# One buffer for the queries: an attention and MLP kernel whose loads and DMA transposes take turns

## The chip, the cores and the metric

The kernel runs on one core of a Trainium2 chip. Five engines work side by side, each on a queue of instructions in a fixed order: TensorE (PE: matmuls, and PEld its weight loads), VectorE (DVE), ScalarE (ACT), GpSimd (POOL) and SyncE (SP). The last two mainly issue DMAs here, which 16 DMA engines then carry out. An engine runs its instructions in order, and each waits for the semaphores that it names. The metric is the device time of one execution in microseconds (us).

## What is computed

The reference, cut to what matters:

```python
def _attn_ref(q, k, v, p):                      # q, k, v: 8 x 8 x 576 x 64; p: 8 x 8 x 32 x 64
    def sm_attn(qq, kk, vv):
        s = scale * np.matmul(qq, kk.transpose(0, 1, 3, 2))
        s = s - np.max(s, axis=-1, keepdims=True)
        a = np.exp(s)
        a = a / (np.sum(a, axis=-1, keepdims=True) + 1e-09)
        return np.matmul(a, vv)
    p_packed = sm_attn(p, k, v)
    return sm_attn(q, p_packed, p_packed)

def _moe_ref(x, w_in, w_out):                   # x: 4608 x 512; w_in: 512 x 2048; w_out: 2048 x 512
    h = x @ w_in
    g = np.where(h >= 1, h, np.where(h <= -1, 0.0, (h + 1) ** 2 / 4.0))
    return g @ w_out
```

For each of 8 batches 32 landmarks `p` first attend to the 576 keys and values, then the 576 queries attend to the 32 packed rows. The output of the 8 heads, side by side, goes through a two-layer MLP.

## The kernel before

The heads' outputs are never written out. The packed rows of a batch are multiplied with `w_in` at once (`mp`, copied to `M`), so that the hidden layer `h` is `M` times the attention weights `A`. One batch goes through these steps: the keys are turned (`kT`), scores `sp` of landmarks and keys and their exponentials `ex`; packed products `pk` with the values; `mp` and `M`; the queries turned (`qT`), scores `s` and exponentials `eT`, their sums, and the weights `A`; then 16 tiles of `h`, each with an `x`, `t` and `hT` step on ACT and DVE; then output tiles `o` of 128 tokens, 16 matmuls each, copied to `ob` and stored. 36 output tiles go through, 9 for each pair of batches. Much of `o` of one pair runs between the steps of the next batches, and so keeps TensorE busy.

Keys and queries of batches 0 and 1 are turned on TensorE (`tp`). From batch 2 on a DMA transposes them from one buffer of SBUF to another, issued from SP (line 562). For batches 5 to 7 the scores are computed with the landmarks on the partitions, and a third DMA transpose turns the exponentials (`exn` to `ex`, line 642). All loads that change the type from f32 to bf16 are issued from POOL (line 411 and others); stores go out from SP (line 1003), in one queue with the transposes.

Four heads of the first keys come another way: `k_raw`, loaded as f32 from SP and ACT (line 458) and cast on DVE and ACT; the landmarks of two batches come as `p_raw` (line 453), cast to `p_nat`, turned on TensorE (`tpp`) and copied to `pT`, which the first scores need.

The buffers are counted in `BUFS`: two for `q`, one each for `k`, `v` and `vv` (the values in pairs of heads, copied on DVE at line 663), two for `kT` and `qT`. Tiles of one tag share its buffers; whoever writes to one waits until those who used it before are done. `p_raw`, the later landmarks `p_late` and the `vv` tiles share the tag `vv`; `k_raw` has the tag `q`.

The order on each engine is written out as numbers: `ORDER` gives a rank (and an engine) to every task of the class `Plan`, which runs through the tasks with its own estimates of their times and from that emits the instructions engine by engine. `add` for a load on POOL carries how long it holds the queue, when it starts and how much it moves; for SP the same for stores and transposes. `chain` lets a task stand behind the one before it. `chain("crossed", t)` keeps the transposes in order, and loads of the weights and of batches 0 and 1 are chained too; the later ones stand as their ranks say. The string `LOADS` and the loop behind it (line 446) make the loads; where the plan leaves TensorE idle early on, `warm` puts matmuls of zeros.

Of the kernel before, what the change touches and what calls it, by code (L numbers as in the profile page):

```python
# [178 lines left out]
def kernel(  # L179
# [54 lines left out]
    o00 35 40 46 49 70 71 73 74 76 81 87 88 94 98 108 111 64A 6
    o01 36 38 44 53 62 93 101 102 112 114 116 117 118 119 122 125 70A 5
    o02 31 50 54 58 59 64 67 69 77 83 85 90 96 100 104 105 65D 2
    o03 41 43 47 56 60 65 68 75 78 82 86 91 95 97 103 107 66D 9
    a1 32 34D 31A 33 35D 36D 79 59D 51A 80 60D 52A 34 33 39 35 63 47A 46A 56 84 53 89 55 57 63 54 92 56 58 64 72 58D
        50A 99 60A 59A
    h1 109 62 69D 70 113 65 71D 73 106 61 67D 68 115 66 72D 74 121 69 76D 78 127 72 79D 83 126 71 77D 84 135 77 79A 86  # L240
        110 63 67A 75 120 68 81D 85 128 73 80D 82 131 74 78A 89 136 80 88D 90 151 82 85A 94 133 76 83A 93 132 75 87A
        95
    o04 138 140 143 144 145 147 155 158 162 163 166 169 172 174 175 177 89A 7
    o05 124 129 130 137 139 146 152 153 156 157 167 179 182 183 184 185 92A 14
    o06 190 196 197 198 203 208 211 216 218 221 222 224 225 228 231 232 111A 13
    o07 186 187 188 189 191 192 193 194 199 200 201 202 204 205 206 207 97A 12
    o08 123 134 141 148 149 150 154 159 161 165 168 170 171 176 178 180 90A 8
    a2 3 4 160 84 164 86 91 92 173 88A 96D 97 181 91 99 101 103 93 100 102 104 98D 195 94A 96A 95A
    h2 209 98 107D 109 214 102 105A 115 210 99 108D 112 215 103 114D 117 220 106 118D 120 213 101 111D 113 223 108
        124D 126 217 104 116D 119 226 109 122D 127 212 100 110D 123 233 112 119A 132 239 115 129D 131 241 121 122A 133  # L250
        219 107 121D 125 230 114 116A 128 246 120 123A 134
    o10 270 271 272 273 274 275 278 279 280 281 282 295 296 297 303 311 161D 19
    o11 236 237 243 244 249 251 252 253 254 259 261 264 266 268 276 277 141D 17
    o12 227 235 238 242 245 247 248 250 256 257 258 260 262 263 265 267 127A 24
    o13 286 288 290 292 299 300 306 307 308 309 310 312 314 316 318 319 151A 21
    a3 10 11 229 110 234 113 105 106 240 117A 118A 130 255 124 135 137 139 125 136 138 140 126A 269 129A 130A 128A
    h3 291 137 152D 156 287 134 146D 148 302 142 155D 160 283 131 143D 158 284 132 145D 147 294 139 153D 154 301 141
        148A 164 289 135 150D 151 293 138 144A 157 305 145 159D 162 304 143 166D 169 317 149 163D 170 320 150 165D 171
        313 146 153A 167 321 155 156A 172 285 133 136A 149
    o14 326 329 333 335 338 339 341 343 344 350 351 353 355 358 360 363 180D 43  # L260
    o15 403 404 406 407 409 410 411 412 413 416 417 419 420 421 422 423 193A 28
    o16 322 324 325 327 328 330 331 332 334 337 340 342 345 346 347 348 160A 23
    o17 369 370 374 375 376 382 384 387 389 391 392 393 395 398 399 400 199D 26
    o18 352 354 356 357 359 362 364 367 373 378 383 388 405 408 414 415 190A 33
    a4 15 16 298 140 315 147 142 144 323 154A 152A 168 336 157 173 175 176 159 174 177 178 158A 349 163A 162A 161A
    h4 379 173 178A 202 371 169 185D 187 402 185 187A 207 368 168 186D 194 377 172 189D 191 372 170 171A 190 394 182
        198D 206 390 179 195D 196 366 167 182D 183 385 180 181A 201 381 176 191A 213 365 166 184D 188 396 186 196A 212
        386 177 193D 197 397 183 184A 203 380 174 175A 192
    o20 471 472 474 476 480 482 483 485 489 490 491 494 496 498 500 502 224A 37
    o21 463 468 473 479 484 486 487 492 493 497 499 501 503 505 506 507 226A 36  # L270
    o22 428 429 430 431 433 438 440 441 443 444 450 454 458 460 465 466 211A 31
    o23 424 425 426 427 432 434 436 437 439 442 445 446 448 449 452 456 218D 32
    a5 18 20 361 164 165 22 179 181 401 189A 188A 205 418 192 208 209 211 194 210 214 215 195A 435 199A 197A 198A
    h5 488 220 236D 237 464 209 223D 226 469 214 230D 231 477 217 221A 235 461 208 221D 222 462 210 227D 229 504 225
        243D 244 451 202 207A 228 470 213 216A 238 455 204 224D 241 453 203 216D 217 459 206 225D 232 478 218 219A 245
        467 212 227A 246 457 205 219D 220 475 215 228A 247
    o24 532 533 534 535 536 539 540 541 542 543 544 545 547 548 549 550 238A 39
    o25 508 509 510 511 516 517 519 520 521 522 523 524 525 526 528 529 232A 38
    o26 512 513 514 515 527 530 537 546 556 574 575 576 577 578 591 592 256A 41
    o27 552 553 554 555 557 559 560 562 563 566 567 568 569 570 571 572 246A 40  # L280
    o28 579 584 585 586 589 593 595 600 602 603 605 609 610 614 619 621 270A 42
    a6 25 27 447 200 201 29 200 204 481 242D 240D 239 518 229 248 249 253 231 250 252 257 230A 573 264D 248A 247A
    h6 561 243 261D 263 565 244 262D 269 564 245 266D 278 558 242 265D 267 587 254 274D 276 588 258 279D 283 594 257
        277D 281 590 255 260A 280 596 259 264A 284 601 262 282D 287 582 251 270D 272 608 265 289D 290 583 252 273D 275
        617 268 269A 293 580 249 268D 271 618 273 295D 299
    o30 625 626 629 634 635 641 642 643 644 645 646 648 650 651 653 661 284A 45
    o31 652 654 655 657 659 660 662 663 666 673 675 676 678 680 681 683 288A 46
    o32 597 599 607 612 613 615 616 622 624 627 630 631 636 637 639 647 279A 44
    o33 665 667 668 669 670 671 672 674 677 679 682 684 685 686 687 689 290A 47
    a7 30 34 495 222 223 35 233 234 531 233A 234A 251 538 236 256 258 259 235 254 255 260 237A 551 239A 240A 241A  # L290
    h7 598 261 285D 292 640 277 302D 303 638 278 309D 312 606 263 286D 288 649 287 310D 314 658 285 311D 313 623 272
        281A 306 628 280 283A 307 656 282 286A 316 632 275 297D 301 581 250 253A 296 611 266 298D 300 633 276 304D 305
        604 267 274A 308 620 271 291D 294 664 289 315D 317
# [778 lines left out]
```

## Time and profile before

| | |
|---|---|
| three runs | 240.09, 243.59, 240.09 us (median 240.09) |
| profiled execution | 242.46 us, of which the span of its instructions 240.7 |
| granted TensorE clock | 0.999 |
| queue of POOL's loads | 18.25 MB, packets took 51.9% of the 16 engines' span |
| queue of SP's and ACT's DMAs | 17.93 MB, 37.5% |
| output matmuls `o` (line 977) | 608, busy 145.4 us |
| hidden matmuls `h` (line 894) | 512, busy 78.3 us |

The profile is one execution. "Busy" of a matmul counts from its issue to its modelled end, and neighbours overlap; so the share of busy time is high even where matmuls come a little apart, and the pace is read from the chain, which shows start to start. In the timeline and the chain a row begins with its start and its duration; "[x <-Y]" is idle time of the engine ahead of the row and what ended it. In the tables of DMAs the last number of a row is the median time from issue to landing.

### The profile page before, as it was taken

What the parts mean: (1) busy time and instruction counts of PE and PEld (TensorE: products, weight loads), DVE (VectorE), ACT (ScalarE), POOL (GpSimd) and SP (SyncE); (2) the same over time, 40 slices, a digit from 0 to 9 for tenths busy, and PEclk for the clock granted to TensorE, in tenths of its full rate; (3) what the DMA queues carried; (4) which work ended last, traced back from release to release, by engine and by line L of the source; (5) the groups of instructions that cost most, each with busy time, mean ns of one, the idle gap of its engine ahead of it and who ended that gap; (6) DMA issues with size and microseconds to landing.
All of it is one profiled execution on the core that took longest, in us unless ns stands there. A gap on an engine that the chain in (4) does not pass through costs nothing.

```text
span 240.7 us, 5388 instructions
## 1 busy us (share of the span) xinstructions
PE 234.2 (97%) x2126; PEld 132.2 (55%) x2126; DVE 187.3 (78%) x354; ACT 182.7 (76%) x315; POOL 28.1 (12%) x42
## 2 busy tenths in 40 slices
PE   7999999999999999999999999999999999999994
PEld 2556555466554765476536653664445566654454
DVE  3547988589959898979898899597997998977102
ACT  3577887899777999898989989987769989782000
POOL 8453210200020120040011030000000000000000
PEclk9999999999999999999999999999999999999999
DMA  7999999999999999999999979998711110222133
GB/s 157 188 205 208 204 205 206 202 212 207 146 176 246 169 171 230 167 181 198 185 147 176 225 134 191 219 222 157 154 46 44 44 46 5 82 88 71 45 81 112
DMA packets 62505, 37.01 MB, mean 154 GB/s; under 512 B 34576, under 2 KB 58000, under 8 KB 62480
## 3 DMA queue, kind: packets, MB, share of 16 engines
q0 software_dynamic: 23104, 18.25, 51.9%
q1 hardware_dynamic: 38832, 17.93, 37.5%
q10 hardware_dynamic: 544, 0.49, 0.7%
q8 instruction: 16, 0.26, 0.4%
q14 instruction: 9, 0.07, 0.1%
HBM read 37.22 MB, written 9.44 MB: 194 GB/s over the span
## 4 chain that ended last, share of the span: by engine, by line
PE 84%; DMA 9%; ACT 2%; POOL 2%; issue 1%; DVE 1%; SPq 0%; ACTq 0%; DVEq 0%; POOLq 0%
PE o L977 49%; PE h L894 24%; DMA w_in_sb<-in_moe_w_in_dram 5%; DMA out_dram<-ob 4%; PE mp L747 3%; PE pk L680 2%; PE sp L590 1%; PE o L1036 1%; PE s L761 1%; POOL q L411 1%; ACT t L910 1%; PE tp L533 1%; PE pk L695 1%; ACT ob L328 1%; ACT M L328 0%
## 5 line engine op out<-in xcount | busy, mean ns | idle before, releaser
L977 PE MATMUL o<-w_out_sb,hT 128*128 128x512 bf16 (+2 forms) x608 | 145.4, 370 | 0.7 <-DVE hT L915 0.3
L915 DVE SCALAR_TENSOR_TENSOR hT<-t 128x576 bf16<-128x576 f32 (+1 forms) x130 | 92.2, 743 | 7.1 <-ACT t L910 6.4
L900 ACT ACTIVATE x<-h 128x576 f32<-128x576 f32 (+1 forms) x130 | 78.4, 644 | 12.2 <-PE h L894 9.9
L977 PEld LDWEIGHTS <-hT 128*128 128x128 bf16 x608 | 56.2, 98 | 54.1 <-issue 7.0
L894 PE MATMUL h<-A,M 128*128 128x288 bf16 x512 | 78.3, 288 | 0.1
L894 PEld LDWEIGHTS <-M 128*128 128x128 bf16 x512 | 50.1, 98 | 26.4 <-ACT M L328 0.7
L908 DVE TENSOR_SCALAR t<-x 128x576 f32<-128x576 f32 (+1 forms) x88 | 38.1, 452 | 12.1 <-ACT x L900 11.0
L328 ACT COPY ob<-o 128x512 f32<-128x512 f32 x26 | 15.2, 586 | 20.0 <-PE o L977 18.4
L328 ACT CAST M<-mp 128x1024 bf16<-128x1024 f32 (+1 forms) x28 | 26.7, 1002 | 2.9 <-PE mp L747 2.9
L910 ACT ACTIVATE t<-x 128x576 f32<-128x576 f32 (+1 forms) x42 | 28.1, 675 | 0.4
L328 DVE COPY ob<-o 128x512 f32<-128x512 f32 (+2 forms) x12 | 7.2, 599 | 14.0 <-PE o L977 14.0
L411 POOL DMA_DIRECT2D k<-in_k_dram x8 | 6.4, 802 | 76.6 <-DMA kT<-k 71.4
L815 DVE SCALAR_TENSOR_TENSOR A<-eT,rs,rc 128x576 bf16<-128x576 bf16 (+1 forms) x18 | 12.7, 732 | 2.8 <-ACT rc L810 2.6
L784 ACT ACTIVATE eT<-s,rs 128x576 bf16<-128x576 f32 x16 | 11.5, 739 | 2.4 <-PE s L761 2.4
L1036 PE MATMUL o<-zeros 128*128 128x512 bf16 (+1 forms) x42 | 12.1, 408 | 1.2 <-DVE zeros L365 1.2
L747 PE MATMUL mp<-w_in_sb,ppT 64*32 64x512 bf16 x256 | 10.8, 382 | 0.1
L411 POOL DMA_DIRECT2D q<-in_q_dram x10 | 7.5, 753 | 18.5 <-PE tp L533 11.6
L595 ACT ACTIVATE ex<-sp 96x768 bf16<-96x768 f32 (+1 forms) x12 | 8.3, 698 | 1.8 <-PE sp L590 1.5
L794 DVE TRANSPOSE_TENSOR_REDUCE r<-eT 128x18 f32<-128x576 bf16 x12 | 9.1, 755 | 0.3 <-ACT eT L784 0.3
L800 DVE STREAM_TRANSPOSE rc<-r 128x576 f32<-128x576 f32 x12 | 8.9, 754 | 0.1
L328 DVE CAST M<-mp 128x1024 bf16<-128x1024 f32 (+1 forms) x5 | 5.6, 1118 | 4.1 <-PE mp L747 4.1
L411 POOL DMA_DIRECT2D v<-in_v_dram x8 | 6.4, 794 | 13.7 <-DVE vv L663 12.2
(62 smaller groups left out, 113.3 us busy)
## 6 DMA issues: line engine op xcount, KB each, us to landing
v<-in_v_dram POOLq DMA_DIRECT2D x8, 576.0 KB, 11.2
out_dram<-ob SPq DMA_DIRECT2D x23, 192.0 KB, 3.3
k<-in_k_dram POOLq DMA_DIRECT2D x7, 576.0 KB, 9.6
q<-in_q_dram POOLq DMA_DIRECT2D x7, 576.0 KB, 11.9
out_dram<-ob SPq DMA_DIRECT2D x24, 128.0 KB, 2.4
w_out_sb<-in_moe_w_out_dram POOLq DMA_DIRECT2D x4, 512.0 KB, 19.5
w_in_sb<-in_moe_w_in_dram POOLq DMA_DIRECT2D x3, 512.0 KB, 15.1
out_dram<-ob SPq DMA_DIRECT2D x23, 64.0 KB, 3.0
```

What stands on the lines that cost most here:

```text
L328: i = (nc.vector.tensor_copy if e == "DVE" else nc.scalar.copy)(to, of)
L411: G_.dma_start(tokens(nm, b)[:, heads(hs)], rows_of(nm, b, hs))
L747: m = nc.tensor.matmul(have["mp", b, f][a * NP:(a + 1) * NP, g], have["ppT", b][r, g, a], w_in_sb[r, a, f * FW:(f + 1) * FW], start=True, ...
L784: nc.scalar.activation(have["eT", b, g], have["s2", b, g][:, :, :HALF], AF.Exp, scale=rs_of[b][:, g, 1:])
L815: V.scalar_tensor_tensor(have["A", b][:, g, xs], have["eT", b, g][:, xs], rs_of[b][:, g, :1], have["rc", b, g][:, xs], ALU.mult, ALU.mult)
L894: nc.tensor.matmul(have["h", b, fi][:, hf, :HALF], have["M", b][:, g, fi * P:(fi + 1) * P], have["A", b][:, g, hf], start=(g == 0), stop=( ...
L900: nc.scalar.activation(have["x", b, fi][:, hs[0]:hs[-1] + 1], have["h", b, fi][:, hs[0]:hs[-1] + 1, :HALF], AF.Prelu, bias=-1.0, alpha=0.5)
L908: V.tensor_scalar(t, x, 1.0, 0.0, ALU.add, ALU.max)
L910: nc.scalar.activation(t, x, AF.Relu, bias=1.0)
L915: V.scalar_tensor_tensor(dst, t, 1.0, t, ALU.min, ALU.mult)
L977: m = nc.tensor.matmul(have["o", key][:, :w], hT[:, fi, i * P:(i + 1) * P], w_out_sb[:, fi, cols], start=(fi == 0), stop=(fi == KF - 1))
L1036: nc.tensor.matmul(o[:, :w], zeros[:, :P], zeros[:, :w], start=True, stop=True)
```

## The change

The queries get one buffer in place of two, and `k_raw` moves from the queries' tag to `vv`. From batch 2 on every load stands in one chain, in the order queries, values, keys, behind which come the transposes of keys and queries. The identity is no longer held behind the first load of keys. The planner's numbers for SP's transposes, for two loads and for the start are new (how long a transpose takes, what share it leaves to loads beside it), and the whole table `ORDER` is new.

```diff
-        self.free = defaultdict(float, DMA=1.75)
+        self.free = defaultdict(float, DMA=1.95)
...
-            return [(a[0], 1.0 - b[0][3]), (b[0], b[0][3])]
+            return [(a[0], 0.5 if b[0][3] < 0.4 else 1.0 - b[0][3]), (b[0], b[0][3])]
...
-    MB0 = {("k", 0, 4): 0.70, ("v", 0, 0): 1.25, ("q", 0, 0): 0.5}
+    MB0 = {("k", 0, 4): 0.75, ("v", 0, 0): 1.35, ("q", 0, 0): 0.5}
...
     ORDER = """
-    first 0 0 0 1 1D 0A
-    load 0 1 2 3 4 5 6 7 8 9 10 11 12 13 14 15 16 21 17 18 19 22 20 23 26 25 27 24 28 29 30 31 32 34 33 35
+    first 0 0 0 1 0A 1D
+    load 0 1 2 3 4 5 6 7 8 9 10 11 12 13 14 15 16 17 18 19 20 21 22 23 24 25 26 27 28 29 30 31 32 33 34 35
...
-    BUFS = dict(w=3, o=2, k=1, q=2, v=1, vv=1, kT=2, qT=2, ex=2, ks=2, ppT=2, M=2, A=2, eT=4, ln=2, rc=2, x=4, t=4, ob=4)
+    BUFS = dict(w=3, o=2, k=1, q=1, v=1, vv=1, kT=2, qT=2, ex=2, ks=2, ppT=2, M=2, A=2, eT=4, ln=2, rc=2, x=4, t=4, ob=4)
...
-    k_raw = work.tile([TP, 4, NC * D], f32, tag="q", name="k_raw", bufs=BUFS["q"])
+    k_raw = work.tile([TP, 4, NC * D], f32, tag="vv", name="k_raw", bufs=BUFS["vv"])
...
-        if key[0] == "p" or "w" in key[0] or key[1] < 2:
-            chain("load", t)
+        chain("load", t)
...
-        for nm in "kqv" if b == 3 else "qkv":
+        for nm in "qvk":
             load(nm, b)
-
-    identity.behind += landed["k", 0, 4]
...
-    k_first = plan.add("first", {"SP": (1.0, 4.2, load_k_raw)})
-    p_first = plan.add("first", {"SP": (0.5, 3.6, load_p_raw)}, behind=[k_first])
+    k_first = plan.add("first", {"SP": (1.0, 4.9, load_k_raw)})
+    p_first = plan.add("first", {"SP": (0.5, 5.1, load_p_raw)}, behind=[k_first])
...
-            t = plan.add(mine, {"SP": (2.9, 0.0, turn, 3.9, 0.9, 0.27)}, landed[nm, b, 0], [nm + "T"])
+            t = plan.add(mine, {"SP": (3.0, 0.0, turn, 2.4, 1.2, 0.2)}, landed[nm, b, 0], [nm + "T"])
...
-            t = plan.add(mine, {"SP": (1.45, 0.0, turn, 2.1, 0.9, 0.27)}, [ready["ex0"], ready["ex1"]], ["ex"])
+            t = plan.add(mine, {"SP": (1.5, 0.0, turn, 1.6, 1.2, 0.2)}, [ready["ex0"], ready["ex1"]], ["ex"])
```

Three lines fewer stand in the file, so a line of the second half carries a number that is 3 lower after the change.

The head of SP's queue, with what each instruction waits for. DMAHW is the landing of a DMA from SP or ACT, DMASW that of one from POOL; the other names are engines. Before:

```order
L458 DMA k_raw<-in_k_dram 96x2x384
L453 DMA p_raw<-in_p_dram 128x256
L1003 DMA out_dram<-ob 32x512 [waits DVE_49]
L1003 DMA out_dram<-ob 96x512
L562 DMA_TRANSPOSE kT<-k 128x24x96 [waits DMASW3_49,PE_49,Activation_49]
L562 DMA_TRANSPOSE qT<-q 128x24x96 [waits DMASW1_49,PE_49,Activation_49]
```

The same queue after the change:

```order
L455 DMA k_raw<-in_k_dram 96x2x384
L450 DMA p_raw<-in_p_dram 128x256 [waits DMAHW0_49,DMAHW1_49,DVE_49,Activation_49]
L559 DMA_TRANSPOSE kT<-k 128x24x96 [waits DVE_49,DMASW4_49,PE_49,Activation_49]
L559 DMA_TRANSPOSE qT<-q 128x24x96 [waits DVE_49,DMASW2_49,PE_49,Activation_49]
L1000 DMA out_dram<-ob 96x512 [waits Activation_49]
L1000 DMA out_dram<-ob 32x512
```

`p_raw` waited for nothing; now it waits for both loads of `k_raw` and for both engines that cast it. The first two transposes stand ahead of the first store.

The loads on POOL from the queries of batch 1 on. Before:

```order
L411 DMA q<-in_q_dram 96x8x384 [waits DMAHW2_49,DMAHW0_49,DMASW7_49]
L428 DMA w_out_sb<-in_moe_w_out_dram 128x4x512 [waits DMASW0_49]
L411 DMA q<-in_q_dram 96x8x384 [waits DMASW1_49,PE_49]
L433 DMA p_late<-in_p_dram 128x3x256 [waits DMAHW1_49,DMASW2_49,DVE_49]
L411 DMA k<-in_k_dram 96x8x384 [waits DMASW3_49,PE_49]
L411 DMA q<-in_q_dram 96x8x384 [waits DMASW7_49,DMASW4_49,PE_49]
L411 DMA v<-in_v_dram 96x8x384 [waits DMASW5_49]
L411 DMA k<-in_k_dram 96x8x384 [waits DMAHW5_49,DMASW6_49,DMASW3_49]
```

After:

```order
L410 DMA q<-in_q_dram 96x8x384 [waits DMASW7_49,PE_49]
L427 DMA w_out_sb<-in_moe_w_out_dram 128x4x512 [waits DMASW0_49]
L410 DMA v<-in_v_dram 96x8x384 [waits DMASW5_49,DMASW1_49,PE_49]
L410 DMA q<-in_q_dram 96x8x384 [waits DMASW7_49,DMASW2_49,PE_49]
L432 DMA p_late<-in_p_dram 128x3x256 [waits DMAHW1_49,DMAHW0_49,DMAHW2_49,DMASW3_49,DVE_49]
L410 DMA k<-in_k_dram 96x8x384 [waits DMASW4_49]
L410 DMA q<-in_q_dram 96x8x384 [waits DMAHW4_49,DMASW2_49]
L410 DMA v<-in_v_dram 96x8x384 [waits DMASW6_49,DMASW1_49,DVE_49]
L410 DMA k<-in_k_dram 96x8x384 [waits DMAHW3_49,DMASW4_49]
```

The values of batch 2 stand ahead of its queries and keys. The queries of batch 3 waited for TensorE's turning of an earlier batch; now they wait for a DMA from SP, the transpose of the queries of batch 2. Before, the keys of batch 3 were asked for ahead of its values (queries of batch 3, values of batch 2, keys of batch 3); now its queries, values and keys stand together. From there on the three follow each other so to the end.

More of the change, by code (lines that the diff above doesn't have):

```diff
@@ L234 @@
[L234 to L241, printed above, removed]
-        95
@@ L243 @@
[L243 to L293, printed above, removed]
@@ new lines @@
+    o00 33 34 41 50 66 73 74 78 87 93 98 100 119 121 125 126 70A 4
+    o01 31 43 48 56 57 62 68 80 82 88 90 91 92 95 101 109 67D 19
+    o02 37 44 46 53 58 59 70 71 72 79 81 85 103 105 106 107 66D 6
+    o03 32 35 40 52 63 64 75 77 86 96 99 104 108 111 112 113 61A 5
+    a1 36 35D 32A 38 36D 33A 83 50A 59D 84 60D 51A 39 34 45 36 67 51D 48A 54 89 52 94 54 56 64 53 97 55 57 65 76 56D
+        49A 102 59A 58A
+    h1 116 64 73D 75 110 60 68D 69 115 63 72D 74 114 62 70D 71 120 67 76D 79 124 71 74A 84 122 68 78D 81 123 73 82D 85
+        118 66 69A 80 136 76 78A 89 128 72 83D 87 117 65 77D 88 134 75 90D 92 150 82 84A 94 142 79 86A 96 137 77 81A
+        95
@@ new lines @@
+    o04 146 147 149 152 153 156 157 159 164 165 168 170 174 176 177 178 88A 12
+    o05 127 129 133 135 139 145 148 155 158 160 169 171 173 179 180 181 99D 7
+    o06 183 184 188 201 203 210 213 217 219 220 221 222 226 229 230 232 111A 17
+    o07 190 191 192 193 194 195 196 197 198 199 200 202 204 205 206 207 95A 11
+    o08 130 131 132 138 140 143 144 151 154 162 163 166 172 185 186 187 91A 10
+    a2 2 3 161 83 167 85 91 93 175 87A 97D 98 182 89 101 103 105 90 102 104 106 100D 189 94A 93A 92A
@@ new lines @@
+    h2 214 100 104A 118 216 102 119D 122 209 97 110D 112 215 101 115D 121 218 103 123D 126 211 98 113D 116 224 106
+        120D 129 223 105 107A 124 228 109 125D 127 212 99 114D 117 208 96 109D 111 240 116 131D 134 227 110 120A 135
+        233 112 128D 130 225 108 115A 132 244 117 121A 136
+    o10 231 235 237 239 242 246 248 249 251 252 261 265 269 275 276 279 129A 16
+    o11 268 270 271 272 273 274 277 278 280 285 286 289 292 293 294 295 152D 18
+    o12 238 241 243 247 250 253 255 256 257 258 259 260 262 263 264 266 125A 13
@@ new lines @@
+    o13 299 302 303 305 306 308 309 311 314 315 320 321 322 323 324 325 155A 22
+    a3 8 9 234 113 236 114 107 108 245 119A 118A 133 254 122 137 139 141 123 138 140 142 124A 267 128A 127A 126A
+    h3 288 135 153D 154 281 130 145D 146 287 134 136A 156 290 138 141A 158 284 133 149D 150 283 132 147D 148 282 131
+        151D 157 296 139 146A 163 317 152 168D 171 310 147 149A 167 291 137 155D 162 312 148 164D 165 300 144 151A 170
+        298 142 161D 166 319 153 156A 172 297 140 159D 160
+    o14 345 348 349 350 351 353 355 356 359 362 363 365 367 368 369 370 185D 25
@@ new lines @@
+    o15 397 398 400 402 403 405 406 412 414 416 417 418 419 420 421 422 191A 28
+    o16 304 316 318 326 327 328 329 332 334 336 337 338 339 340 341 343 160A 21
+    o17 331 333 335 342 346 347 352 354 377 378 381 385 387 389 391 392 181A 27
+    o18 374 379 382 383 386 394 396 399 404 407 409 410 411 413 415 425 192A 44
+    a4 14 15 301 143 307 145 143 144 313 150A 154A 169 330 157 173 175 177 158 174 176 178 159A 344 161A 162A 163A
+    h4 366 170 194D 195 376 174 175A 201 372 172 191D 192 357 164 182D 188 358 165 180D 184 380 176 196D 198 361 167
+        189D 193 388 182 185A 203 360 166 183D 186 375 179 197D 200 393 184 204D 208 373 173 178A 205 401 186 195A 216
+        384 177 206D 218 390 180 190A 214 371 171 187D 190
@@ new lines @@
+    o20 471 472 474 476 479 480 481 483 486 494 495 497 498 500 503 505 223A 36
+    o21 473 475 477 482 485 487 489 490 492 496 499 501 502 504 506 507 222A 34
+    o22 424 426 427 428 429 430 432 434 435 437 441 443 448 452 454 461 209A 37
+    o23 431 433 436 438 439 440 442 445 446 450 455 457 462 463 465 466 229D 31
+    a5 20 23 364 168 169 24 179 181 395 183A 202D 199 408 187 207 210 213 188 209 211 215 189A 423 194A 212D 193A
+    h5 467 208 213A 236 484 217 241D 242 488 221 245D 247 464 207 218A 248 456 202 225D 226 449 199 223D 235 491 219
+        244D 246 460 206 231D 232 453 201 203A 227 451 200 222D 224 458 204 228D 239 447 198 220D 221 470 211 237D 251
+        459 205 230D 238 493 220 249D 252 468 210 226A 257
@@ new lines @@
+    o24 576 577 581 582 583 584 585 586 589 592 594 595 597 598 601 602 254A 42
+    o25 542 543 545 546 547 549 551 552 554 556 557 558 562 563 568 569 240A 40
+    o26 509 510 511 515 517 519 522 524 526 530 532 540 541 544 548 553 262D 39
+    o27 512 513 514 516 518 520 521 525 527 528 529 531 534 535 537 538 230A 38
+    o28 559 560 561 564 565 566 570 571 572 573 579 588 596 604 605 606 256A 41
+    a6 26 29 444 196 197 30 217 219 469 233D 212A 234 478 216 240 243 254 214 250 253 255 215A 508 224A 229A 225A
@@ new lines @@
+    h6 539 233 261D 272 536 231 234A 271 590 248 249A 283 575 242 273D 277 599 253 284D 286 578 244 245A 275 533 232
+        270D 274 614 260 292D 293 600 255 288D 289 591 250 280D 282 593 251 285D 291 580 246 276D 278 587 247 252A 281
+        616 261 267A 297 574 243 279D 290 608 259 262A 294
+    o30 611 615 618 619 626 627 629 630 635 637 639 640 641 642 643 644 273A 43
+    o31 609 610 612 613 622 623 625 628 633 634 650 651 655 657 663 664 311D 45
+    o32 647 648 649 653 654 656 658 660 661 662 666 668 673 676 678 680 284A 46
@@ new lines @@
+    o33 669 670 671 672 674 675 677 679 681 682 683 684 685 686 687 689 286A 47
+    a7 32 33 523 227 228 35 258 259 550 235A 260D 256 555 236 263 264 268 238 265 267 269 237A 567 241A 239A 266D
+    h7 636 272 302D 303 659 278 280A 312 652 277 309D 310 645 279 314D 318 631 268 270A 299 638 271 304D 306 665 281
+        283A 316 620 263 264A 295 617 276 307D 313 632 269 287A 319 607 257 296D 317 624 265 298D 301 603 258 287D 300
+        646 274 308D 315 667 282 285A 320 621 266 275A 305
+    o34 725 726 727 730 731 732 733 736 738 739 740 741 743 744 745 747 321D 50
@@ L300 @@
+    o35 694 695 698 699 700 701 702 703 705 706 707 708 711 714 715 716 288A 49
+    o36 721 722 723 724 728 729 734 735 737 742 746 748 749 750 751 752 322D 51
+    o37 688 690 691 692 693 696 697 704 709 710 712 713 717 718 719 720 289A 48
+    o38 753 754 755 756 757 758 759 760 761 762 763 764 765 766 767 768 323D 52 769 770 771 772 773 774 775 776 777
+        778 779 780 781 782 783 784 324D 53 785 786 787 788 789 790 791 792 793 794 795 796 797 798 799 800 325D 54
     """
```

18 lines of the change are left out of this document (6 added, 12 removed).

## The prediction

> **What bounds the kernel now.** I read the page's engine rows first, then the stretches of 10 us, the chain that ended last, the timeline of the first 31 us, and the DMA tables.
>
> ```profile
> PE 234.2 (97%) x2126; PEld 132.2 (55%) x2126; DVE 187.3 (78%) x354; ACT 182.7 (76%) x315; POOL 28.1 (12%) x42
> DMA  7999999999999999999999979998711110222133
> GB/s 157 188 205 208 204 205 206 202 212 207 146 176 246 169 171 230 167 181 198 185 147 176 225 134 191 219 222 157 154 46 44 44 46 5 82 88 71 45 81 112
> ```
>
> TensorE is busy for 97% of the span: it is the bound. But the DMA engines are full too, until slice 28 (170 us). So a change of the transfers can hardly gain, since TensorE has nearly no idle time to give back, and it can lose, as soon as a transfer comes after the matmul that needs it. How little there is to gain after the start:
>
> ```profile
> 150.00:160.00 10.00, 9.66 (x80) 6.22 (x80) 7.04 (x14) 8.94 (x18) 0.00 (x0) 1.00 1.27 205
> 170.00:180.00 10.00, 9.65 (x109) 4.37 (x106) 9.66 (x20) 7.10 (x13) 0.00 (x0) 1.00 0.42 107
> ```
>
> The number behind the stretch's length is TensorE's busy time. From 30 to 230 us these two alone stand below 10.00, together 0.69 us. Now the chain (start, duration, what):
>
> ```profile
> 61.75 1.80 PE o L977 x8
> 69.06 0.70 PE pk L680 x24
> 84.72 0.49 PE h L894 x4
> 92.91 1.73 PE o L977 x8
> 162.02 0.70 PE pk L680 x24
> 175.00 0.70 PE pk L680 x24
> ```
>
> It shows two things. The packed products of keys (pk) of batch 2 start at 69.06, of batch 7 at 175.00, 105.9 us for five batches. And 8 output matmuls took 1.80 us at 62 us, but 1.73 at 93: 225 ns and 216 ns each. The profiled execution took 242.46 us (span 240.7 and 1.8 around it), the median of the three runs 240.09. Some 60 us (20 to 80) at 216 for 225 would be 2.4 us shorter, which is the distance between the two; so I take 2.4 us off the sum at the end. The Trainium skill (TensorE: Matmul & The Clock Gate, "Wait — 56ns, not 53.3ns?") gives 215.7 ns from one matmul of 512 columns to the next at the full clock: the row at 93 us agrees, the one at 62 does not, though the granted clock reads 1.00 in both. By the page's pace, which I estimate from that figure, the same 2.4 us come off.
>
> **Part 1, the start.** `k_raw` moves into the buffer of `p_raw`, so the load of the landmarks (`p_raw`) now waits until both casts of `k_raw` are done. The timeline of before:
>
> ```profile
> 1.18 0.43 SPq L453 DMA_DIRECT2D p_raw<-in_p_dram  x1
> 2.07 0.22 POOL masks.py:197 MEMSET ident<- 128x128 bf16 x1
> 2.37 0.29 POOL masks.py:199 TENSOR_SCALAR_AFFINE_SELECT ident<-ident 128x128 bf16<-128x128 bf16 x1
> 5.05 0.83 ACT L328 CAST k<-k_raw 96x768 bf16<-96x768 f32 x1 [3.03 <-DMA k_raw<-in_k_dram]
> 5.27 0.29 DVE L508 CAST p_nat<-p_raw 128x256 bf16<-128x256 f32 x1 [0.19 <-DMA p_raw<-in_p_dram]
> 5.62 0.28 PE L479 MATMUL tpp<-ident,p_nat 128*128 128x128 bf16 x2
> 5.95 1.09 ACT L328 COPY pT<-tpp 64x128 bf16<-64x128 bf16 x4
> 8.34 0.70 ACT L328 COPY kT<-tp 128x288 bf16<-128x288 bf16 x2 [1.30 <-PE tp L533]
> 8.92 0.50 ACT L595 ACTIVATE ex<-sp 96x384 bf16<-96x384 f32 x1
> 9.86 1.41 ACT L595 ACTIVATE ex<-sp 96x384 bf16<-96x384 f32 x3 [0.44 <-PE sp L590]
> 11.46 0.94 PE L685 MATMUL pk<-ex,v 96*64 96x32 bf16 x48
> 19.42 0.41 PE L894 MATMUL h<-A,M 128*128 128x288 bf16 x2
> ```
>
> Before, `p_raw` was issued at 1.18 and was hidden behind the keys. Now it is issued when the cast on ScalarE ends, 5.05 + 0.83 = 5.9. How long it takes there no row shows; the nearest are
>
> ```profile
> out_dram<-ob SPq DMA_DIRECT2D x24, 128.0 KB, 2.4
> p_raw<-in_p_dram SPq DMA_DIRECT2D x1, 128.0 KB, 4.1
> ```
>
> a store of the same size beside loads (2.4) and its own load behind `k_raw` in one queue (4.1). I take 3.0, nearer to the store since nothing is ahead of it in its queue. So it lands at 8.9. Behind it VectorE waits with the cast in its order, and with it the copies of the turned keys; on TensorE the turned landmarks and all that follows. From 8.9: cast 0.29, transposes 0.28, four pT copies 1.09, one kT copy 0.4 (half of 0.70 rounded up), four exponentials 0.50 + 1.41 = 1.9. That ends at 12.9, where before it ended at 9.86 + 1.41 = 11.3: **1.6 us later** (1.0 with 2.4, 2.7 with 4.1), and `pk` follows at once. The identity is made ahead of the first load on the POOL queue: 0.22 + 0.29 us later for `k`, at no cost, since the keys' second half stands behind `tpp` on TensorE, which is now later than that; without `p_raw`'s wait it would cost up to 0.5.
>
> Not all of the 1.6 arrives. The first phase then waits for weights, which come by their own queue:
>
> ```profile
> 12.44 1.55 POOL L423 DMA_DIRECT2D w_in_sb<-in_moe_w_in_dram  x2 [0.33 <-DMA q<-in_q_dram]
> 30.32 0.41 PE L747 MATMUL mp<-w_in_sb,ppT 64*32 64x512 bf16 x8
> DMA to landing us min/median/max: 9.6/13.0/16.8
> ```
>
> (the last row is that of `w_in_sb`.) The second of these loads is issued at 13.25 and takes the 16.8, so it lands at 30.05 and its matmuls start at 30.32. The queue was full at 205 GB/s all the while, so it lands there now too. TensorE's work up to there shifts into that wait. Between nothing and all of 1.6 I take half: **+0.8**.
>
> **Part 2, the loads in a ring.** With one buffer, the queries of a batch are asked for only when the batch before has been transposed, values and keys stand behind them on the POOL queue, and the transposes behind the keys on SP. What hid this before was the second buffer. Rows for one turn (waits; then landings of loads, of kT, qT, ex):
>
> ```profile
> POOL k L411 <- DMA kT<-k: 71.4, 5, 15.8
> DMA to landing us min/median/max: 6.5/9.9/21.2
> DMA to landing us min/median/max: 6.3/8.4/11.8
> DMA to landing us min/median/max: 5.0/7.2/15.9
> DMA to landing us min/median/max: 4.2/7.5/8.6
> L562 SPq DMA_TRANSPOSE kT<-k x6: 3971/6118/7343, 50.8 to 155.5; - x6
> 140.24 5.49 SPq L562 DMA_TRANSPOSE qT<-q x1
> 147.78 10.37 DMA out_dram<-ob
> L625 ACT ACTIVATE exn<-s 128x576 bf16<-128x576 f32 x6 | 3.9, 652 | 0.4 <-PE s L618 0.3
> ```
>
> Transposes beside loads are slow: the one of 140.24 is the 15.9 us, against 5.0 alone, and a store behind it took 10.4. That goes. In the ring, with the fastest rows because transposes and loads no longer meet: first load 6.5, two more of 576 KB at 205 GB/s 2.9 each, then kT, whose issue holds SP for 4.0, and qT, which lands 5.0 after it, 0.5 for semaphores: 6.5 + 5.8 + 4.0 + 5.0 + 0.5 = **21.8 us**. A batch's stores, some 4.5 tiles of 256 KB, are 5.8 us at that rate; most of them fit where the ring itself moves nothing (about 5 us at the starts), so I take 22.3 (21.8 to 27.6).
>
> TensorE's side: in the new order 286 output matmuls and 268 of `h` stand between pk of batch 2 and of batch 7, before 273 and 256. At 216 and 123 ns (four of `h` in 0.49, at 84.72) that is 94.7 for 90.5 us; with the other 15.4 of the 105.9 it makes 110.1, or 22.0 per batch: the ring turns as fast as it is used. The tightest place is the scores of batch 5, 152 output matmuls and 144 of `h` behind those of batch 2: 50.5 + 9.3 = 59.8 us for three turns, 66.9. The lead is what the first turn leaves:
>
> ```profile
> 30.65 0.81 POOL L411 DMA_DIRECT2D k<-in_k_dram  x1 [1.84 <-DMA w_in_sb<-in_moe_w_in_dram]
> 50.81 5.95 SPq L562 DMA_TRANSPOSE kT<-k  x1
> 65.69 0.54 PE L590 MATMUL sp<-pT,kT 128*128 128x64 bf16 x12
> ```
>
> The keys of batch 2 landed just ahead of 50.81 and now have the values ahead of them, 2.9 later; their transpose, 6.3, ends at 60.0; the scores come at 65.7 + 0.8: 6.5 us. So 66.9 - 59.8 - 6.5 = 0.6 us of waiting at batch 5. Third, the transposes of the exponentials: from the scores to pk of batch 6 there are 13 output matmuls and 44 of `h`, 8.2 us. In them must lie two exponentials of 0.65, some 0.8 for the matmuls ahead of them and the hand-overs (my choice), and a transpose of 4.2 alone or 7.5 beside the next loads: 6.3 to 9.6, so 0 to 1.4 late, 0.9 taken. Together **+1.5**. Against it the 0.69 of idle time falls away, since slow transposes end: **-0.7**. The planner's new numbers (1.95, 2.4 and the like) set only the order, and cost nothing themselves; the last tiles of the program are cut as before.
>
> **Sum.** 242.46 + 0.8 + 1.5 - 0.7 = 244.1 in the profiled execution's terms, less 2.4: **241.7 us**, against a median of 240.09.
>
> **Rivals.** *Slower: the ring is slower than its user.* If the stores do not fit and a turn takes 23.5, batch 5 waits 70.5 - 66.3 = 4.2 us in place of 0.6, and batches 6 and 7 some 0.75 more each: 241.7 + 3.6 + 1.5 = 246.8. It decides from a turn of about 23. For it: no slack of 22.3 against 22.0, and a full DMA. Against it: a turn of before, kT at 50.81 to the last at 155.5, took 20.9 on average with slow transposes in it. The Trainium skill (DMA: Bandwidth & Descriptors, "Rules for kernel authors") says to issue a DMA early and wait for it late, so that its fixed cost overlaps with work; the change does the opposite for the queries, and by that rule this rival is the outcome. No run here shows yet what it costs; the long landings in the rows above are what overlap costs in this kernel.
>
> *Hidden anyway.* The start is absorbed, all transfers are in time, the idle 0.7 goes: 242.46 - 0.7 - 2.4 = 239.4. For it: a queue that is full until 50 us, and a lead of 6.5. Against it: the order's own step towards `p_raw`.
>
> *Nothing absorbed.* `p_raw` takes 4.1 and all 2.7 arrive: 241.7 + 1.9 = 243.6.
>
> **How the numbers follow.** 2% of 240.09 is 4.8 us, about what a measurement of this kernel can tell from no change. Forecast 0.39, nothing absorbed 0.10, hidden anyway 0.22, the slower ring 0.26, and 0.03 for a gain over 2%, for which the profile has no place: slower 0.26, faster 0.03, the same 0.71. The time is that of the likeliest, 241.7. The range goes from 238.6, a little below the hidden case, up to 247.5, a little above a turn of 23.5; a turn of 25 and more lies outside.
>
> **What would show it.** Right: `p_raw` is issued at 5 to 6 us and lands at 8 to 9; the first pk at 12.5 to 13.5; queries, values and keys of a batch are issued within some us of each other and kT lands in 6 to 7 us; pk of batch 7 at 178 to 182. Wrong: an idle TensorE before the scores of batch 5 or pk of batch 6 of over 3 us (the ring), or a first `h` (19.42 before) that comes no later (part 1). A landing of transposes beside loads as long as before would break part 2.

## The result and the profile after

| | before | after |
|---|---|---|
| runs | 240.09, 243.59, 240.09, 241.09 us | 251.63, 252.24, 255.29, 254.62 us |
| median | 240.59 us | 253.43 us |
| profiled execution (span) | 242.46 us (240.7) | 251.63 us (249.8) |

The changed kernel is slower: 1.0507 times the time before, 95% interval 1.0381 to 1.0633. (A ratio counts, of each kernel, the runs that lie close to its fastest, so it is not quite that of the two medians.) All four of its runs lie above the forecast range.

The page of the profile after the change: TensorE's row, the granted clock and the DMA engines' share in 40 slices of 6.2 us.

```profile
PE 233.9 (94%) x2090; PEld 134.6 (54%) x2125; DVE 188.8 (76%) x359; ACT 179.5 (72%) x310; POOL 28.7 (12%) x42
PEclk9869999999999999999999999799999999999999
DMA  7999999698999899798969996999796203023134
```

TensorE is busy for the same 234 us as before, in a span that is 9 us longer: it did not get more work, it waits. (Some of its matmuls are missing from this trace, 33 of `o`; all 608 of their weight loads are in it.) The DMA engines, which were full up to slice 28, now have a dent in every turn of the ring (a 6, a 7 or an 8 among the nines). The waits of TensorE, longest first (total us, how often, the longest one):

```profile
PE s L615 <- DMA kT<-k: 4.4, 3, 2.0
PE tpp L476 <- DVE p_nat L505: 4.3, 1, 4.3
```

No other is longer than 1.2. Both rows are new, and they are the two parts of the change: the landmarks at the start (`p_nat`, cast from `p_raw`), and the turned keys of batches 5, 6 and 7 (`s`). First the start, from the timeline:

```profile
5.20 0.36 SPq L450 DMA_DIRECT2D p_raw<-in_p_dram  x1
10.94 0.29 DVE L505 CAST p_nat<-p_raw 128x256 bf16<-128x256 f32 x1 [5.83 <-DMA p_raw<-in_p_dram]
11.29 0.39 PE L476 MATMUL tpp<-ident,p_nat 128*128 128x128 bf16 x2 [4.26 <-DVE p_nat L505]
17.96 0.94 PE L682 MATMUL pk<-ex,v 96*64 96x32 bf16 x48
```

`p_raw` was issued at 5.20, within the forecast 5 to 6, but its cast starts only at 10.94, and the first `pk` comes at 17.96 where it came at 11.46. Then the ring: the start-to-start distance of the six transposes of keys, and one turn of SP's queue.

```profile
L559 SPq DMA_TRANSPOSE kT<-k x6: 2907/3032/3562, 59.0 to 177.6; - x6
```

The six go from 59.0 to 177.6, so a turn takes 118.6 / 5 = 23.7 us on average; before, from 50.8 to 155.5, it took 20.9. Single turns on SP's timeline and on the chain:

```profile
59.03 2.95 SPq L559 DMA_TRANSPOSE kT<-k  x1
...
103.63 3.56 SPq L559 DMA_TRANSPOSE kT<-k  x1
...
127.25 3.08 SPq L559 DMA_TRANSPOSE kT<-k  x1
130.44 1.96 SPq L1000 DMA_DIRECT2D out_dram<-ob  x4
132.50 3.42 SPq L559 DMA_TRANSPOSE qT<-q  x1
```

```profile
132.50 5.34 DMA qT<-q
139.91 11.82 DMA k<-in_k_dram
151.78 4.88 DMA kT<-k
156.71 0.44 PE s L615 x16
177.64 5.07 DMA kT<-k
```

The first two turns took (103.63 - 59.03) / 2 = 22.3 us each, the next ones 23.6, 24.5 and 25.9. TensorE's scores follow the landing within 0.05 us (151.78 + 4.88 = 156.66, the scores at 156.71): it stands waiting for it. The stretches in which it does so, with TensorE's busy time as the number behind the length and the granted clock third from the right:

```profile
130.00:140.00 10.00, 8.61 (x71) 5.28 (x70) 7.95 (x15) 7.46 (x15) 1.61 (x3) 1.00 1.00 193
150.00:160.00 10.00, 7.91 (x62) 3.50 (x48) 6.66 (x11) 5.12 (x10) 0.00 (x0) 0.86 0.71 140
180.00:190.00 10.00, 8.91 (x71) 4.51 (x71) 5.32 (x10) 6.39 (x12) 0.00 (x0) 1.00 1.00 202
```

The account: the start comes 17.96 - 11.46 = 6.5 later and the waits of `s` are 4.4, together 10.9 us. The two profiled executions are 9.2 apart, and 11 to 11.6 apart without the 1.8 to 2.4 us (an estimate, worked out below) that the one before lost to its slower pace. The account leaves out what the wait in the second stretch cost beyond itself: the granted clock was 0.86 there.

### The profile page after: what moved, and what is told of

The parts are those of the page before. It is cut to its first block, busy times and chain, and to the rows that moved or that the text cites. A ratio compares the mean times of both kernels' runs of the same rounds, so it can differ in the third digit from the quotient of the medians.

```text
span 249.8 us, 5351 instructions
## 1 busy us (share of the span) xinstructions
PE 233.9 (94%) x2090; PEld 134.6 (54%) x2125; DVE 188.8 (76%) x359; ACT 179.5 (72%) x310; POOL 28.7 (12%) x42
## 4 chain that ended last, share of the span: by engine, by line
PE 77%; DMA 17%; issue 1%; ACT 1%; DVE 1%; POOL 1%; SPq 0%; POOLq 0%; ACTq 0%
PE o L974 42%; PE h L891 23%; DMA kT<-k 6%; DMA k<-in_k_dram 5%; PE o L1033 3%; PE mp L744 3%; DMA p_raw<-in_p_dram 2%; DMA qT<-q 2%; PE sp L587 2%; DMA k_raw<-in_k_dram 2%; PE pk L677 1%; PE tp L530 1%; PE s L758 1%; ACT x L897 1%; PE s L615 0%
## 5 line engine op out<-in xcount | busy, mean ns | idle before, releaser
L974 PE MATMUL o<-w_out_sb,hT 128*128 128x512 bf16 (+2 forms) x575 | 138.1, 369 | 2.0 <-issue 0.6
L907 ACT ACTIVATE t<-x 128x576 f32<-128x576 f32 x43 | 29.4, 687 | 0.5
L328 ACT CAST M<-mp 128x1024 bf16<-128x1024 f32 (+1 forms) x26 | 25.0, 1002 | 2.5 <-PE mp L744 2.5
L328 ACT COPY ob<-o 128x512 f32<-128x512 f32 x25 | 14.6, 589 | 15.3 <-PE o L974 13.0
L328 DVE COPY ob<-o 128x512 f32<-128x512 f32 (+2 forms) x13 | 7.8, 608 | 15.5 <-PE o L974 15.2
L1033 PE MATMUL o<-zeros 128*128 128x512 bf16 (+1 forms) x39 | 13.6, 481 | 1.3 <-DVE zeros L365 1.2
L328 DVE CAST ppT<-pk 64x128 bf16<-64x128 f32 x12 | 3.5, 289 | 7.8 <-PE pk L677 4.0
L328 DVE CAST M<-mp 128x1024 bf16<-128x1024 f32 (+1 forms) x7 | 8.0, 1147 | 0.9 <-PE mp L744 0.8
```

Of the source, the lines that this page charges most:

```text
L328: i = (nc.vector.tensor_copy if e == "DVE" else nc.scalar.copy)(to, of)
L907: nc.scalar.activation(t, x, AF.Relu, bias=1.0)
L974: m = nc.tensor.matmul(have["o", key][:, :w], hT[:, fi, i * P:(i + 1) * P], w_out_sb[:, fi, cols], start=(fi == 0), stop=(fi == KF - 1))
L1033: nc.tensor.matmul(o[:, :w], zeros[:, :P], zeros[:, :w], start=True, stop=True)
```

## The experiments

The two theories behind them: the loss is the start, late by all of `p_raw`'s delay; and the ring, whose turn is longer than TensorE's. Each kernel is compared with the one before, run beside it on the same chip: a median, then the ratio with its 95% interval. "Own buffer" below is the changed kernel with `k_raw` in a buffer of its own, from which four others start.

### The start undone (e1_own_k)

```diff
-    k_raw = work.tile([TP, 4, NC * D], f32, tag="vv", name="k_raw", bufs=BUFS["vv"])
+    k_raw = work.tile([TP, 4, NC * D], f32, tag="kr", name="k_raw", bufs=1)
```

> The changed kernel, with a buffer of its own for k_raw, so that p_raw waits for nothing. Theory A (two costs that add: 6 us at the start from p_raw, 6 to 7 us from the ring of loads and transposes): about 247.5 us, the first pk at 11.5 to 12.5 us in place of 18.0, and TensorE still idle before the scores of batches 5 to 7, by as much or up to 2 us more. Rival B (only the ring counts, and a late start merely takes the place of waiting there): 251 to 253 us, with the idle time before those scores longer by some 5 us.

249.98 us, ratio 1.0361 (1.0255 to 1.0468). The transposes of keys and TensorE's waits:

```profile
L559 SPq DMA_TRANSPOSE kT<-k x6: 2933/2986/3036, 55.3 to 176.2; - x6
```

```profile
PE s L615 <- DMA kT<-k: 6.5, 3, 2.8
PE o L974 <- ACT ob L328: 2.4, 1, 2.4
```

The wait for the landmarks is gone and the first turn starts 3.7 us earlier, yet only 1.5 of the 5.1 points come back, between what the two theories gave. The turn is 24.2 us long, and what TensorE gains at the start it now waits for in the ring: 6.5 us in place of 4.4, and 2.4 more for an output tile whose store stood behind a transpose. Ring and start are partly in one another's shadow.

### The start alone (e4_before_shared)

The kernel before, with only `k_raw` moved:

```diff
-    k_raw = work.tile([TP, 4, NC * D], f32, tag="q", name="k_raw", bufs=BUFS["q"])
+    k_raw = work.tile([TP, 4, NC * D], f32, tag="vv", name="k_raw", bufs=BUFS["vv"])
```

> The kernel before the change, with k_raw in the buffer of p_raw and nothing else. Theory A: the start costs the same in it, 245 to 247 us, the first pk 5 to 7 us later than 11.46. Rival E (the late start is absorbed where the first phase waits for weights, and the loss belongs to the ring alone): 240 to 243 us.

249.15 us, ratio 1.0313 (1.0228 to 1.0399). TensorE's wait and the packed products of batch 7 on the chain:

```profile
PE tpp L479 <- DVE p_nat L508: 6.6, 1, 6.6
```

```profile
182.23 0.70 PE pk L680 x24
```

The wait is 6.6 us. The first `pk` starts at 19.11, 7.7 us late, and pk of batch 7 comes 7.2 us after the 175.00 of before, which had itself lost some 2 us to its pace by then: none of the delay is absorbed on the way. Alone, the start costs 3.1 points; the ring alone (e1) costs 3.6; both together 5.1.

### Why `p_raw` is slow (e9_p_alone)

```diff
             def emit(e, hs=hs):
+                if (nm, b) == ("v", 0):
+                    hold = work.tile([128, 8], f32, tag="hold", name="hold", bufs=1)
+                    G_.tensor_copy(hold, p_raw[:, 0, :8])
                 G_.dma_start(tokens(nm, b)[:, heads(hs)], rows_of(nm, b, hs))
```

> The changed kernel, but the loads behind the first keys (values, queries, weights) are held on POOL until p_raw has landed (a small copy of p_raw on POOL stands ahead of them), so that only the keys' second half moves beside p_raw. Theory: p_raw took 5.7 us because its packets stand behind those of six loads that POOL had already issued; then it is issued at 5.2 as before and now lands within 2.5 to 3.5 us, at 8 to 9, and the first scores are correspondingly earlier. Rival: the latency of a load issued there is 5 us or more in any company; then it lands at 10 to 11 again. The whole time says nothing on this, since all other loads are some 4 to 6 us later: 253 to 260.

`p_raw` landed 2.1 us after its issue at 5.46, sooner than expected, and the first `pk` came at 14.1. (One run, 252.31 us; the time says nothing on this, since all other loads come later.) The DMAs of the 3.6 us behind the issue of `p_raw` in the changed kernel, and then of the 2.2 us behind that (queue, kind, packets, MB, share of 16 engines; POOL's loads are the software queue, SP's and ACT's DMAs the hardware one):

```profile
q0 software_dynamic: 871, 0.66, 124.9%
```

```profile
q0 software_dynamic: 478, 0.35, 104.6%
q1 hardware_dynamic: 144, 0.13, 22.1%
```

The same for the 2.2 us behind its issue when only the first keys are ahead of it, and the landing:

```profile
q0 software_dynamic: 138, 0.09, 28.4%
q1 hardware_dynamic: 144, 0.13, 20.8%
```

```profile
DMA to landing us min/median/max: 2.1/2.1/2.1
```

The 0.13 MB are `p_raw`. In the changed kernel not one of its packets moved in the first 3.6 us, while 871 packets of loads issued by POOL did. Without those loads its first packet moved after some 0.9 us, and it was through in 2.1. So the price of this load was set by the loads that POOL had issued, although they came by another queue. (The run holds back both their packets and POOL's work of issuing them, so it does not tell these two apart.) The Trainium skill (DMA: Bandwidth & Descriptors, "Queues, rings and completion order") says that each engine goes round the queues that have work, packet by packet; by that rule `p_raw` would have had its share from about 0.9 us on. Here it did not: 871 to 0 in 3.6 us. Only then did its packets go between POOL's, 144 beside 478, as the page has it.

### TensorE kept warm at the start (e8_warm)

The plan is told that `p_raw` takes 9.9 us, so that it puts 20 more matmuls of zeros into the wait:

```diff
-    p_first = plan.add("first", {"SP": (0.5, 5.1, load_p_raw)}, behind=[k_first])
+    p_first = plan.add("first", {"SP": (0.5, 9.9, load_p_raw)}, behind=[k_first])
```

> The changed kernel (251.6 to 255.3 us) with some 20 more matmuls of zeros on TensorE while it waits for p_raw, so that it isn't idle there; the wait itself stays. Theory I (part of the late start is TensorE's lower clock behind 4.5 us of idling: granted 0.83 over the first 20 us): the first pk 0.5 to 1.5 us earlier than 18.0, 251 to 253 us. Rival: no difference, the chain from p_raw runs on VectorE and ScalarE.

251.99 us, ratio 1.0468 (1.0403 to 1.0534), which can't be told from the change's 1.0507. Here are the first 20 us of the changed kernel and of this one, and the end of the wait with the first `pk`:

```profile
0.00:20.00 20.00, 14.45 (x151) 8.80 (x152) 6.16 (x26) 6.66 (x16) 11.04 (x21) 0.83 1.09 186
```

```profile
0.00:20.00 20.00, 17.74 (x196) 9.35 (x198) 7.19 (x30) 7.73 (x17) 12.36 (x22) 1.00 1.09 186
```

```profile
11.88 0.29 PE L476 MATMUL tpp<-ident,p_nat 128*128 128x128 bf16 x2 [0.57 <-DVE p_nat L505]
16.13 0.94 PE L682 MATMUL pk<-ex,v 96*64 96x32 bf16 x48
```

The wait of 4.3 us had cost the clock too, 0.83 in place of 1.00. From the transposed landmarks to `pk` it is 16.13 - 11.88 = 4.3 us here and 17.96 - 11.29 = 6.7 there: 2.4 us of the start's 6.5 went with the clock, not with the load. (In this stretch there are also 10 matmuls of zeros in place of 12, which may account for a few tenths. `p_raw` came later here, so `pk` gains 1.8.) Most of that did not reach the end, since `s` then waited 5.4 us for the ring in place of 4.4.

### A shorter turn (e5_q_eighth, e10_q_half)

Own buffer, with less to load in each turn:

```diff
             for i, hs in enumerate({("k", 0): [range(4, 8)], ("q", 0): Q0}.get((nm, b), [range(H)])):
+                if nm == "q" and b > 2:
+                    hs = range(1)
                 def emit(e, hs=hs):
+                    if nm == "q" and b > 2:
+                        have["q", b] = have["q", 2]
```

In the second of them it is `range(4)`.

> As the run with a buffer of its own for k_raw (250.0 us), but from batch 3 on the load of the queries brings one head of eight; the seven others stay those of batch 2, so the output is that of other queries. All waits and the order on every engine are the same; only a turn of loads and transposes becomes shorter, by about 2.5 us (from 23.9 on average, keys' transpose to keys' transpose, to 21.4). Theory A (TensorE waits because a turn takes longer than its 22 us per batch): the idle time before the scores of batches 5 to 7 (6 us in all there) goes, 243 to 246 us. Rival F (those scores wait for something else that the new order holds late, stores or copies): 248 us or more.

> The kernel with k_raw in a buffer of its own (249.98), in which from batch 3 on the load of the queries brings 4 heads of 8; the transposes, orders and waits are the same, and the output is partly of other queries. With one head of 8 the turn was 21.7 us on average from kT to kT and the time 239.8, with all 8 it was 23.9 and 250.0. Theory (the time goes with the length of the turn as soon as it is longer than about 22): a turn of 22.7 to 23.0 and 243 to 247. Rival (any full ring costs the same, the eighth was a special case of transposes that land earlier): 248 to 251. Rival (the waits vanish with the first saved microsecond): 239 to 241.

With one head 239.83 us, ratio 0.9954 (0.9893 to 1.0016); with four 242.98 us, ratio 1.0078 (1.0037 to 1.0120). The transposes of keys with one head, and with four heads together with the wait for them:

```profile
L564 SPq DMA_TRANSPOSE kT<-k x6: 2905/3014/3672, 54.7 to 164.9; - x6
```

```profile
L564 SPq DMA_TRANSPOSE kT<-k x6: 2959/3019/3617, 54.2 to 171.1; - x6
```

```profile
PE o L979 <- ACT ob L328: 2.4, 1, 2.4
...
PE s L620 <- DMA kT<-k: 1.1, 1, 1.1
```

| queries loaded per turn | turn, issue to issue | TensorE waits for kT | time |
|---|---|---|---|
| one head | 22.0 us | none over 0.2 us | 239.83 us |
| four heads | 23.4 us | 1.1 us | 242.98 us |
| eight heads | 24.2 us | 6.5 us | 249.98 us |

(The expectation counts from landing to landing, where the first is 21.7. Turns and waits are those of the profiled executions, which took 239.37, 245.03 and 250.08 us: with four heads that is 2 us above the median. With four and with eight heads TensorE also waited 2.4 us once for an output tile whose store came late.) The time follows the length of the turn, and steeply so between 23 and 24 us. The edit also takes bytes off the DMA engines, up to 0.5 MB in each of five batches; a turn shortened without that was not found in the experiments below. The first row also shows what the new order is worth where the ring doesn't hold it up: 0.9954, not told from no change.

### The second buffer back (e2_two_q, e3_old_bufs)

The first is the changed kernel with two buffers for the queries, the second has also `k_raw` back in their tag, so that all buffers are as before and only the order and the order of loads are new:

```diff
-    BUFS = dict(w=3, o=2, k=1, q=1, ...
+    BUFS = dict(w=3, o=2, k=1, q=2, ...
```

> The changed kernel with two buffers for the queries again, k_raw still in the buffer of p_raw, order of every engine unchanged. Theory A: the queries of the next batch load while those of this one are transposed, a turn is some 3 us shorter, the idle time before the scores of batches 5 to 7 goes: 246 to 248 us, the transpose of the keys of batch 7 lands before 172 us (182.7 now). Rival D (values and keys behind the queries are held by the copies of the values or by stores, or transposes beside loads lose what the earlier load wins): over 251 us, kT of batch 7 still after 178.

> The changed kernel with both buffers as before the change (two for the queries, k_raw in one of them); the new order and the order of the loads stay. Theory A: both costs gone, 240 to 243 us. Rival C (the new order of the engines or of the loads is itself a cost): over 245 us, with idle time on TensorE at places that the changed kernel has too.

262.44 us, ratio 1.0839 (1.0714 to 1.0964), and 259.87 us, ratio 1.0715 (1.0571 to 1.0859): theory A fails in both, and both are slower than the change itself. Rival D holds in the first, where the keys of batch 7 are turned at 184.87 only. SP's timeline and TensorE's waits in the first:

```profile
81.87 4.30 SPq L559 DMA_TRANSPOSE kT<-k  x1
86.28 7.81 SPq L559 DMA_TRANSPOSE qT<-q  x1
94.19 4.13 SPq L1000 DMA_DIRECT2D out_dram<-ob  x6
```

```profile
PE o L974 <- ACT ob L328: 6.2, 2, 5.1
...
PE pk L677 <- DMA ex<-exn: 4.9, 1, 4.9
```

With a second buffer the loads start while the transposes run: here the values, at 84.21. The transpose at 86.28 then holds SP for 7.81 us, where that of the same batch took 3.09 in the changed kernel, and the stores behind it come late: output tiles wait for a free `ob`, `pk` waits for `ex`. So the turn-taking does keep transposes short, and this order, made for it, is slower without it.

### Queries turned ahead of the stores (e6_q_behind)

Own buffer, with `qT` right behind `kT` in batches 5 and 6, ahead of the four stores that stand between them:

```diff
-    a5 20 23 364 ...
+    a5 20 20.5 364 ...
...
-    a6 26 29 444 ...
+    a6 26 26.5 444 ...
```

> As the run with a buffer of its own for k_raw (250.0 us), and in batches 5 and 6 the transpose of the queries stands right behind that of the keys on SP, with the four stores that stood between them behind it. Theory A: kT to landed qT takes 8 us in place of 10.6 to 12.3 in these two batches, so the keys of batches 6 and 7 come 2.5 and up to 4 us earlier, and of the 4 us that TensorE waits there 2 to 4 go: 246 to 248 us. Rival G (stores that come later hold up the copies of the outputs and TensorE as much): 249.5 to 251.

257.52 us, ratio 1.0678 (1.0584 to 1.0771), against 1.0361 without this. SP's timeline and the queries' next load on POOL:

```profile
125.58 3.04 SPq L559 DMA_TRANSPOSE kT<-k  x1
128.72 3.12 SPq L559 DMA_TRANSPOSE qT<-q  x1
...
134.17 1.83 SPq L639 DMA_TRANSPOSE ex<-exn  x1
```

```profile
134.42 0.77 POOL L410 DMA_DIRECT2D q<-in_q_dram  x1 [20.31 <-DMA qT<-q]
```

The landings of the two transposes of exponentials there, what waits for them, and the landings without the edit:

```profile
DMA to landing us min/median/max: 10.8/11.2/11.7
```

```profile
PE pk L677 <- DMA ex<-exn: 7.9, 2, 6.6
```

```profile
DMA to landing us min/median/max: 3.7/4.1/4.6
```

The loads are issued 1.9 us earlier (134.42 for 136.31), beside the transpose of exponentials, which then takes 11 us in place of 4. The edit also puts the four stores right ahead of that transpose, but its packets still moved fast behind them: from 135.5 to 136.0 us 323 packets went on the hardware queue (418 without the edit), and only from 136.0 to 136.5 did they fall to 82 (415 without it). The place of `qT` behind the stores had kept the loads away from it. In this order the turn was not to be shortened from that side.

### Keys loaded first (e7_keys_first)

Own buffer, with the loads of each batch in the order keys, queries, values:

```diff
-        for nm in "qvk":
+        for nm in "kqv":
```

> As the run with a buffer of its own for k_raw (250.0 us), but from batch 3 on the loads stand in the order keys, queries, values. So the next keys load beside the transpose of the queries, and the transpose of the keys runs beside the loads of queries and values. Theory H (from the run with two buffers: a transpose beside loads holds SP for 6 to 8 us and the stores behind it come late): slower, 253 to 260 us, kT and qT 8 to 12 us to landing. Theory A taken alone (the length of the keys' turn is all that counts): faster, 244 to 247 us.

248.10 us, ratio 1.0196 (1.0099 to 1.0292), against 1.0361 (1.0255 to 1.0468): some better, though the intervals overlap. Two of the runs took 245.23 and 246.03 us, in the range of theory A, and two 250.17 and 250.66, between the two theories. The profile is that of 250.66. The landings of five of the transposes of keys in it:

```profile
DMA to landing us min/median/max: 5.4/11.6/15.3
```

The keys need not wait for the queries' transpose any more, so their load starts earlier; but their transpose now lies beside the loads that follow, and takes 11.6 us in the middle, as theory H has it. Whether it does so in the two shorter runs too is not shown, and so neither theory is decided; how much of the gain and of the loss reaches the end was not taken apart.

## Why the prediction was wrong

**The price of `p_raw`, 3.0 us between 2.4 and 4.1.** It was issued within the forecast time, but took 5.7 (6.1 in e4, 6.3 in e8). The lower bound was a misreading: 2.4 is the median of 24 stores, taken for stores "beside loads". Most of those ran without any. In the profile before, first those from 50 to 80 us, with loads under way, then those from 165 us on, with none left:

```profile
out_dram<-ob SPq DMA_DIRECT2D x4, 128.0 KB, 6.2
```

```profile
out_dram<-ob SPq DMA_DIRECT2D x14, 128.0 KB, 2.4
```

Over the whole profile the 27 stores issued with a load under way took 6.5 us in the median (3.3 to 12.1), the 49 others 2.3. So 2.4 is the price without loads, and the stores beside loads were near the 5.7 that came. The upper bound, 4.1, was the load's own time at 1.18, when only the two loads of `k_raw` had been issued ahead of it; at 5 us it has the loads of POOL ahead of it, and e9 shows that they are the cause. The upper bound was no bound.

**The steps behind it, 4.0 us to `pk`.** They took 7.0 from 10.94 to 17.96. The durations were read where TensorE ran at the full clock; 2.4 us of the difference went with the clock (e8), which the wait had lowered.

**Half of the delay absorbed.** None was. The prediction read the matmuls `mp` at 30.32 as a wait for the weights' landing. Their neighbours on TensorE in the kernel before:

```profile
29.78 0.61 PE L977 MATMUL o<-w_out_sb,hT 128*128 128x512 bf16 x2
...
30.66 0.61 PE L977 MATMUL o<-w_out_sb,hT 128*128 128x512 bf16 x2
```

There is no gap ahead of `mp` (the two `o` from 29.78 fill the time up to it), and its row, shown in the prediction, bears no "idle before": output matmuls stood in front of it. A weight that lands just in time is no idle time in which a delay could vanish. Part 1 was forecast at 0.8 and came to 6.5 at the first `pk`.

**A turn of 22.3 us.** Right for the first two turns, to a tenth, and short by 1.3 to 3.6 for the others. At 127.25 the queries' transposes land at 132.50 + 5.34 = 137.84, 10.6 us after the keys' was issued, where 4.0 + 5.0 = 9.0 were reckoned: four stores stand between them (1.96 us). The loads then take from 138.39 to 139.91 + 11.82 = 151.73, 13.3 us for 12.3. The prediction let "most" of the stores fit into the ring's own pauses; in the queue of SP they stand in the ring.

**The waiting, 1.5 us.** Its largest part, 0.9 for the transposes of exponentials, did not come (they landed in 3.7 to 4.3 us, and `pk` waited for none), while batches 5, 6 and 7 waited 4.4 for their keys in place of 0.6. And the late start gave the ring time: without it the same waits were 6.5, and 2.4 more for a store (e1).

**The rival.** "The ring is slower than its user", with a turn of 23.5 and 246.8 us, was the mechanism, at 0.26; it reckoned 5.1 us more than the forecast. The turn of 23.7 is what it said, and the point at which it decides, "from a turn of about 23", is where the table of the shortened turns has it. What it lacked was the start: with a start late by 6.5 in place of 0.8 it would have said 246.8 + 5.7 = 252.5, close to the 253.43 measured, though partly by luck: the two overlap, as the start undone shows. The rule of the Trainium skill on early issue (DMA: Bandwidth & Descriptors, "Rules for kernel authors") gives the right sign for the single buffer, but not the cure: two buffers in this order cost still more.

**What held.** In the ring the transposes of keys land in 4.9 to 5.4 us and those of queries in 5.0 to 6.7, near the 5.0 reckoned, and hold SP for about 3 (4.0 were reckoned for the keys). The pace of the profiled execution before was its own: in the changed kernel the output matmuls follow one another at 216 ns in the median of every 10 us from 30 on. The 2.4 us taken off for it were a little much: before, these medians are 217 ns from 20 to 30 us and 224 from 30 to 80, which by the same estimate makes 50 x 8 / 224 = 1.8 us.

## What to carry to other kernels

A wait counts as cover only where the engine's row shows idle time ahead of it; a transfer that lands just in time, even if the chain passes through it, absorbs nothing. (In the first 24 us of this kernel some of TensorE's work is matmuls of zeros. They stand in its fixed order, so they don't give way either.) For a ring of one buffer, add up every instruction that stands in it on each queue, stores included, and compare with its user's pace: here 22.0 us cost nothing, 23.4 one or two microseconds, 24.2 nearly nine. A load that is moved to a later time is to be priced by what the DMA engines have before them at that time, not by the same load elsewhere, and the clock that TensorE loses in a wait of some 4 us comes on top.

## What the hardware showed that had not been expected

A load of 128 KB from SP moved no packet for 3.6 us while 871 packets of loads from POOL went ahead of it, and landed after 5.7 us; with those loads held back its first packet moved after 0.9 and it landed after 2.1. Whether it is the order of issue, the kind of queue or POOL's work of issuing that decides was not tried. That DMAs from SP are slow beside POOL's loads shows elsewhere too: in the kernel before, a store took 6.5 us in the median with a load under way and 2.3 without (some of the slow ones also stood behind a transpose).

A DMA transpose that meets loads is slowed by much: one of 1.46 us on SP and 3.7 to landing became one of 1.83 and 10.8 when the loads were issued 0.25 us behind it rather than 2.2 us.
